# A filter's results through DRAM: loads of two units in 16 rows of 32 KB, stores in pieces of 512 bytes

## The chip, the core and the metric

The kernel runs on one core of one Trainium2 chip. The metric is the device time of one execution in microseconds. Three runs of the kernel before took 3746.42, 3749.2 and 3750.16 us; the median is 3749.2 us.

## The reference, cut to what matters

The input is one sequence of 2048 rows by 1024 columns. Two kinds of layer alternate, each behind a layer norm and added to its input:

```python
x = x + A(layernorm(x), wqkv, wo)      # attention, 32 heads
x = x + B(layernorm(x), w_r, w_i)      # spectral filter
x = x + A(layernorm(x), wqkv, wo)
x = x + B(layernorm(x), w_r, w_i)

def B(x, w_r, w_i):
    X = rfft2(x, axes=(-2, -1))
    y = irfft2(X * (w_r + 1j * w_i), s=(S, D), axes=(-2, -1))
    return y
```

The change lies in the filter B, which is executed twice.

## The kernel before, in words

Attention (lines 343 to 988) takes most of the time and is not touched. The filter is the function `spectral`, from line 1004. It does the two-dimensional transform by matrix products on TensorE (PE), in three stages.

The first stage (t1 and fa, lines 1034 to 1069) transposes 128-column blocks and multiplies by a matrix that does the small outer factors of the transform at once. Its result lies in SBUF in the buffer of 64 KB per partition that the attention calls big or R (the two change places between the layers).

The second stage is a software pipeline over 32 units, the list UNITS of line 23. A unit is a pair of a column parity g (0 or 1) and a row frequency class k1, with four or five column classes. Units 0 to 15 have g = 0, and units 16 to 31 have g = 1. Iteration i of the loop at line 1216 holds, in this order:

- `fb(i)`, line 1130: the products of the forward row transform (L1122), and the copies of the result from PSUM into a tile B on ScalarE (L1115)
- `halves(i - 2)`, line 1176: ScalarE and VectorE split the filtered unit into two float16 parts, H (L1179, L1180)
- `fc(i - 1)`, line 1144: the forward column transform (L1154), the multiplication with the filter weights on VectorE and GpSimd (L1161 to L1169), and at its end `loadw(i + 2)` (L1089), a load of weights w, 256 KB as a rule
- `binv(i - 3)`, line 1182: the inverse row transform (L1122 again, from H), copied into U by ScalarE (L1115)
- `turn(i - 6)`, line 1207: two loads of 128 KB from the DRAM tensor zt into the tile turned (L1210)
- `cinv(i - 4)`, line 1193: the inverse column transform (L1199, L1202), a copy from PSUM into a tile T on ScalarE (L1204), and the store of T to zt, 256 KB (L1205). There are three buffers of T
- in odd iterations, a load of 512 KB of the residual y (L1235)

Behind the loop stand `turn(30)` and `turn(31)`. In this loop the instructions of PE, ScalarE (ACT) and SyncE (SP) are issued in the order of the code. All loads and stores named here are issued by SyncE, which works through its queue in order: an instruction that has to wait for a semaphore holds up all behind it. VectorE (DVE) and GpSimd (POOL) get their order from the planner.

The way through DRAM is a transposition. In T, a partition stands for (r, q): r is one of two halves, q one of 64 column positions, and each partition holds four column classes j of 128 row positions n. In turned, a partition stands for a row of the third stage's matrix (`row`, line 32: unit, r and j), and holds 64 q of 128 n. The matrix `mi`, made by `spec_consts` at line 36, is laid out by the same function `row`.

The third stage (lines 1246 to 1296) multiplies turned by mi (`ai`, L1249). `even(a)` needs the half with g = 0, `odd(a)` the half with g = 1, so the first `odd` product needs the last loads of zt. VectorE (L1259, L1266, L1267) and GpSimd (L1268) add the results to the residual. In the second filter each of the eight steps stores 1 MB of the output, in pieces of 512 bytes (L1293, L1296). In the first filter the weights of the next attention are loaded and split in between (L312, L218, L219, L321 to L323).

Attention's partial sums go through GpSimd's DMA queue (L765 to L770): transfers of 32 neighbouring partitions, added up in DRAM.

Of the kernel before, what the change touches and what calls it, by code (L numbers as in the profile page):

```python
# [6 lines left out]
F32 = mybir.dt.float32  # L7
# [15 lines left out]
UNITS = [u for g in range(2) for u in  # L23
         [(g, k1, list(range(4 * h, 4 * h + 4))) for k1 in range(1, 8) for h in range(2)]
         + [(g, k1, [0, 1, 2, 3] if g else [1, 2, 3, 0, 4]) for k1 in (0, 8)]]
# [4 lines left out]


def row(i, r, j):
    return 32 * (i % 16 // 4) + 16 * r + 4 * j + i % 4


def spec_consts():
# [967 lines left out]
def spectral(nc, tc, ap, yd, xout, a, cst, zt, fast, flags=None, nxt=None, join=None):  # L1004
# [25 lines left out]
    turned = ap.r.rearrange("p (g q n) -> p g q n", g=2, q=64)  # L1030
# [99 lines left out]
    def fb(i):  # L1130
        g, k1, fs = UNITS[i]
        n = len(fs)
        pb = new_ps(n)
        for j, o, m in PAIRS[n]:
            src = [bh[:, g, i % 16, x] for x in range(2)] if fast else [bu[:, g, i % 16]]
            if j < 2:
                lr, li = ([v[:, r * n + o:r * n + o + m].rearrange("p a q -> p (a q)") for v in src] for r in range(2))
            else:
                lr, li = [v[:, 3:5].rearrange("p a q -> p (a q)") for v in src], None
            complex_mm(pb[j // 2][:64 * m, j % 2].rearrange("p r k -> p (r k)"), lr, li, const("cb", k1))  # L1140
        B = Bt[i] = p2.tile([128, 6, 128], F32, name="B")
        restack(n, pb, B)

    def fc(i):
        g, k1, fs = UNITS[i]
        n = len(fs)
        B, w = Bt.pop(i), W.pop(i)
        G = (p2 if fast else p3).tile([128, 2, 6, 64], F32, name="G")
        H = G if not fast else p3.tile([128, 2, 2, 6, 64], F16, name="H")
        Gt[i] = [H[:, x] for x in range(2)] if fast else [G]  # L1150
        for o, m in GRP[n]:
            pc = ps.tile([128, 4, 2, 64], F32, name="ps")
            for j in range(m):
                nc.tensor.matmul(pc[:, j].rearrange("p r f -> p (r f)"), B[:, POS[n][o + j]], C["cc"][:, 8 * g + fs[o + j]],  # L1154
                                 start=True, stop=True)
            xr, xi = pc[:, :m, 0], pc[:, :m, 1]
            wr, wi = w[:, 0, o:o + m], w[:, 1, o:o + m]
            p0 = POS[n][o]
            gr, gi = G[:, 0, p0:p0 + m], G[:, 1, p0:p0 + m]
            t_ = p1.tile([128, 2, 4, 64], F32, name="t_")  # L1160
            nc.vector.tensor_mul(gr, xr, wr)  # L1161
            nc.vector.tensor_mul(t_[:, 0, :m], xi, wi)
            nc.vector.tensor_mul(gi, xr, wi)
            last = nc.vector.tensor_mul(t_[:, 1, :m], xi, wr)
            if flags is not None and seen and o == 0:
                with tc.issue_after(last.ins):
                    largest(*seen.pop())
            nc.gpsimd.tensor_tensor(gr, gr, t_[:, 0, :m], op=ALU.subtract)
            nc.gpsimd.tensor_tensor(gi, gi, t_[:, 1, :m], op=ALU.add)  # L1169
            if fast:  # L1170
                todo.append([i] + [v[:, :, p0:p0 + m] for v in (G, H[:, 0], H[:, 1])])
        loadw(i + lead)
# [3 lines left out]
    def halves(i):  # L1176
        while todo and todo[0][0] == i:
            _, gs, hi, lo = todo.pop(0)
            nc.scalar.copy(hi, gs)  # L1179
            nc.vector.tensor_sub(lo, gs, hi)  # L1180
# [12 lines left out]
    def cinv(i):  # L1193
        g, k1, fs = UNITS[i]
        n = len(fs)
        U = Ut.pop(i)
        pt = ps.tile([128, 4, 128], F32, name="ps")
        for j in range(4 if n == 4 else 3):
            nc.tensor.matmul(pt[:, j], C["ci"][:, 8 * g + fs[j]], U[:, j], start=True, stop=True)  # L1199
        if n == 5:  # L1200
            for j in range(2):
                nc.tensor.matmul(pt[64 * j:64 * j + 64, 3], C["ci"][:, 8 * g + fs[3 + j], 0:64], U[:, 4 + j], start=True, stop=True)  # L1202
        t_ = p4.tile([128, 4, 128], F32, name="T")
        nc.scalar.copy(t_, pt)  # L1204
        nc.sync.dma_start(zt[i], t_)  # L1205

    def turn(i):
        for r in range(2):
            r0 = row(i, r, 0)
            nc.sync.dma_start(turned[r0:r0 + 13:4, UNITS[i][0]], zt[i][64 * r:64 * r + 64].rearrange("q j p -> j q p"))  # L1210

    for i in range(lead):
        loadw(i)
# [1 line left out]
    with tc.manual_schedule(engines=set(hold)) if fast else nullcontext():  # L1215
        for i in range(36):
            if i < 32:
                fb(i)
            if 0 <= i - 2 < 32 and fast:
                halves(i - 2)  # L1220
            if 0 <= i - 1 < 32:
                fc(i - 1)
            if 0 <= i - 3 < 32:
                binv(i - 3)
            if 0 <= i - 6 < 32:
                turn(i - 6)
            if 0 <= i - 4 < 32:
                cinv(i - 4)
            if i == 20 and join:
                joined = join(ps)  # L1230
            if 20 <= i < 23 and join:
                next(joined, None)
            if i % 2 and i < 32:
                t = i // 2
                nc.sync.dma_start(rest[:, t], yd[t * 128:(t + 1) * 128, :])  # L1235
        turn(30)
        turn(31)
    psum.close()
    work.close()
    mid.close()  # L1240
# [202 lines left out]
def build(nc, tc, a):  # L1443
    with ExitStack() as ctx:
        cp = ctx.enter_context(tc.tile_pool(name="consts", bufs=1))
        dr = ctx.enter_context(tc.tile_pool(name="layers", bufs=1, space=DRAM))
        cst = {n: cp.tile(s, d, name=n) for n, s, d in (
            ("ident", [128, 128], F32), ("ones", [128, 32], F32), ("bones", [128, 32], BF16),
            ("half", [128, 1], F32), ("sign", [128, 1], F32), ("mhalf", [128, 1], F32), ("mi", [128, 2, 128], F32))}
        nc.scalar.dma_start(cst["ident"], a["ident"])  # L1450
        nc.scalar.dma_start(cst["sign"], a["sign"])
        nc.vector.memset(cst["ones"], 1.0)
        nc.vector.memset(cst["bones"], 0.0)
        for h in range(4):
            nc.vector.memset(cst["bones"][32 * h:32 * h + 32, h:h + 1], 1.0)
        nc.vector.memset(cst["half"], 0.5)
        nc.vector.memset(cst["mhalf"], -0.5)
        flags = {
            "mv": cp.tile([128, 32, 2], F32, name="fmv"),
            "w": cp.tile([128, 32], F32, name="fw"),  # L1460
            "wb": cp.tile([128, len(UNITS)], F32, name="fwb"),
            "r": cp.tile([128, 16], F32, name="fr"),
            "st": cp.tile([128, NST, 2, 6], F32, name="fst"),
            "bad": cp.tile([1, 1], I32, name="fi"),
        }
        nc.vector.memset(flags["r"], 0.0)
        x1 = dr.tile([2048, 1024], F32, name="x1")
        zt = dr.tile([32, 128, 4, 128], F32, name="zt")
        ap = AttnPools(tc)
        ap.open_small()  # L1470
        x = a["x"]
        for o in (0, 512):
            nc.sync.dma_start(ap.x[:, 0, o:o + 512], x[0:128, o:o + 512])
        wts = [Weights(nc, ap, a["wp"], True, [flags["w"][:, i:i + 1] for i in range(32)], []),
               Weights(nc, ap, a["wp"], None, [], [])]
        for layer in range(2):
            y = dr.tile([2048, 1024], F32, name=f"y{layer}")
            attention(nc, tc, layer, ap, x, y, wts[layer], a["wo"], cst, dr, flags)
            x = a["out"] if layer else x1
            if layer:  # L1480
                spectral(nc, tc, ap, y, x, a, cst, zt, True, join=lambda ps: combine_flags(nc, ps, cp, flags, cst))
            else:
                spectral(nc, tc, ap, y, x, a, cst, zt, True, flags, (s for ph in PH0 for s in wts[1].prep(ph)))
        ap.close()
        bad = nc.values_load(flags["bad"][0:1, 0:1], min_val=0, max_val=1)
        with tc.If(bad > 0):
            x = a["x"]
            for layer in range(2):
                y = dr.tile([2048, 1024], F32, name=f"gy{layer}")
                general_attention(nc, tc, x, y, a["wp"], a["wo"], cst)  # L1490
                ap = AttnPools(tc)
                load_norm(nc, tc, cst, ap, y)
                x = a["out"] if layer else x1
                spectral(nc, tc, ap, y, x, a, cst, zt, False)
                ap.close()
# [28 lines left out]
```

## Time and profile before

| what | value |
|---|---|
| median of three runs | 3749.2 us |
| the profiled execution's own time | 3747.77 us |
| its span, first to last instruction | 3745.9 us |
| mean granted PE clock | 0.988 |
| PE busy in the span | 97% |
| loads of zt in the two filters, 128 KB each | 64 and 64 |
| stores of T, 256 KB each | 64 |
| second stage, first filter: first matmul to last T copy | 1645.13 to 1831.84 us |
| second stage, second filter: first matmul to last T copy | 3520.89 to 3686.63 us |

The profile is one execution. Its times count from the first instruction of the span. A row of a timeline has the start, the time taken, the engine, the line, the operation, the tiles (out<-in) and how many instructions are merged; in square brackets stands the idle time ahead of it and what ended it. A row of a wait reads: the engine and its line, what it waited for, microseconds in total, number of times, the longest. A DMA share is the mean busy share of the core's 16 DMA engines; it can exceed 1 because a DMA engine works on more than one packet at a time. An issue of a DMA (SPq) is the time for which the queue's engine was busy issuing, not the time of the transfer.

### The profile page before, as it was taken

How to read it: one execution, taken by the hardware profiler on the slowest of the kernel's cores; microseconds unless marked ns; L12 is line 12 of the kernel's file. 1: busy time of each engine (PE TensorE's matmuls, PEld its weight loads, DVE VectorE, ACT ScalarE, POOL GpSimd, SP SyncE). 2: the span in 40 equal slices, each digit the busy share in tenths (PEclk: the TensorE clock that was granted, in tenths of full speed). 3: DMA queues.
4: the chain of work that ended last, by engine and by line, in shares of the span. 5: the costliest groups of instructions: out<-in, count | busy, mean ns of one | idle time of the engine just before them, and what ended most of it. 6: DMA issues, size and time to landing. Idle time of an engine off the chain costs nothing. (4 is left out here: it accounts for less than half of the span.)

```text
span 3745.9 us, 80372 instructions
## 1 busy us (share of the span) xinstructions
PE 3619.1 (97%) x32663; PEld 1600.1 (43%) x32663; DVE 3129.2 (84%) x3754; ACT 2900.8 (77%) x3571; POOL 671.0 (18%) x802
## 2 busy tenths in 40 slices
PE   8999999999999999998689999999999999999995
PEld 5333433443343333487654334333433433333885
DVE  7799899989999979875467998999899889788744
ACT  5788888888888868577447888888888888676782
POOL 1012112211121100124220111111111111000243
PEclk9999999999999999999889999999999999999998
DMA  7122332222233432245451222323222334321465
GB/s 196 21 52 55 54 56 48 60 42 52 55 64 60 95 102 74 81 141 182 140 158 27 52 52 51 55 53 60 44 52 52 63 59 97 102 77 74 145 208 177
DMA packets 245965, 307.74 MB, mean 82 GB/s; under 512 B 77392, under 2 KB 156752, under 8 KB 244560
## 3 DMA queue, kind: packets, MB, share of 16 engines
q1 hardware_dynamic: 206624, 228.49, 19.4%
q0 software_dynamic: 37632, 73.43, 13.7%
q8 instruction: 258, 4.23, 0.5%
q14 instruction: 123, 1.01, 0.1%
q10 hardware_dynamic: 1328, 0.59, 0.1%
HBM read 165.65 MB, written 135.20 MB: 80 GB/s over the span
## 5 line engine op out<-in xcount | busy, mean ns | idle before, releaser
L740 ACT ACTIVATE p<-s,bias 128x1024 f32<-128x1024 f32 x2048 | 2170.9, 1112 | 457.7 <-PE s L736 439.6
L759 DVE TENSOR_TENSOR acc<-acc,p 128x1024 f32<-128x1024 f32 x896 | 1044.0, 1220 | 55.9 <-ACT p L740 54.8
L759 DVE TENSOR_TENSOR big<-big,p 128x1024 f32<-128x1024 f32 x448 | 522.5, 1221 | 38.4 <-ACT p L740 37.2
L759 DVE TENSOR_TENSOR R<-R,p 128x1024 f32<-128x1024 f32 x448 | 522.2, 1220 | 31.4 <-ACT p L740 29.8
L746 PE MATMUL o<-p,big 128*32 128x512 f32 x4096 | 492.5, 598 | 0.0
L746 PE MATMUL o<-p,R 128*32 128x512 f32 x4096 | 492.5, 598 | 0.0
L426 PEld LDWEIGHTS <-wqk 128*128 128x128 f16 x3072 | 275.7, 98 | 418.8 <-issue 127.3
L426 PE MATMUL x<-R,wqk 128*128 128x512 f16 x1440 | 338.1, 380 | 1.9 <-ACT big L488 1.2
L426 PE MATMUL x<-big,wqk 128*128 128x512 f16 x1440 | 338.2, 380 | 1.4 <-ACT R L488 0.7
L736 PEld LDWEIGHTS <-R 32*128 32x128 f16 x6144 | 114.8, 92 | 370.6 <-issue 312.8
L736 PEld LDWEIGHTS <-big 32*128 32x128 f16 x6144 | 114.2, 92 | 370.2 <-issue 312.0
L746 PEld LDWEIGHTS o<-p,R 128*32 128x32 f32 x4096 | 106.8, 109 | 261.7 <-issue 261.7
L746 PEld LDWEIGHTS o<-p,big 128*32 128x32 f32 x4096 | 106.8, 109 | 261.7 <-issue 261.7
L736 PE MATMUL s<-R 32*128 32x512 f16 x3072 | 213.8, 377 | 0.1
L736 PE MATMUL s<-Q,big 32*128 32x512 f16 x3072 | 212.7, 377 | 1.0 <-DVE mqk L460 1.0
L736 PE MATMUL s<-Q,R 32*128 32x512 f16 x3072 | 212.6, 378 | 1.0 <-DVE mqk L460 1.0
L736 PE MATMUL s<-big 32*128 32x512 f16 x3072 | 212.6, 377 | 0.1
L765 POOL DMA_DIRECT2D zd<-acc x112 | 92.4, 825 | 650.7 <-DVE z L775 304.2
L484 PE MATMUL x<-wv,big 128*128 128x256 f16 x1392 | 166.7, 276 | 3.0 <-DVE R L219 2.2
L484 PEld LDWEIGHTS <-big 128*128 128x128 f16 x1536 | 146.2, 99 | 49.7 <-issue 28.6
L484 PE MATMUL x<-wv,R 128*128 128x256 f16 x1392 | 165.7, 275 | 0.7 <-ACT R L392 0.7
L484 PEld LDWEIGHTS <-R 128*128 128x128 f16 x1536 | 145.7, 98 | 46.7 <-issue 26.1
(524 smaller groups left out, 4158.6 us busy)
## 6 DMA issues: line engine op xcount, KB each, us to landing
zd<-acc POOLq DMA_DIRECT2D x112, 256.0 KB, 4.1
wst<-in_wp SPq DMA_DIRECT2D x96, 256.0 KB
zt<-T SPq DMA_DIRECT2D x64, 256.0 KB
w<-in_w SPq DMA_DIRECT2D x60, 256.0 KB
zd<-R POOLq DMA_DIRECT2D x56, 256.0 KB, 4.1
zt<-zr SPq DMA_DIRECT2D x224, 64.0 KB
od<-ohl SPq DMA_DIRECT2D x56, 256.0 KB
zd<-big POOLq DMA_DIRECT2D x56, 256.0 KB, 4.1
```

Of the source, the lines that this page charges most:

```text
L426: nc.tensor.matmul(ps, a, b, start=i == 0, stop=i == 23)
L484: nc.tensor.matmul(ps[:, j], x[c][:, d, o:o + 128], w[:, n, d], start=i == 0, stop=i == 23)
L736: nc.tensor.matmul(s[h // 2][:, h % 2], K[g][r, a, kt * 128:kt * 128 + 128], Q[g][r, b, c * 512:c * 512 + 512], start=i == 0, stop=i == 2)
L740: nc.scalar.activation(p, s[hf], AF.Exp, bias=bias[g], scale=SCALE / (SQ * SQ))
L746: nc.tensor.matmul(O[g, c][32 * h:32 * h + 32], V[g][:, kt, 32 * h:32 * h + 32], P[g, c, kt, h // 2][:, h % 2], start=kt == 0, stop=kt == ...
L759: last_add = nc.vector.tensor_add(a, a, p)
L765: nc.gpsimd.dma_start(z, a[32 * j:32 * j + 32].rearrange("p a j n -> p (a j n)"), max_dma_last_dim=2048, **({"accum_op": ALU.add} if j els ...
```

## The change

In zt, the class j now stands ahead of the partition p. A store therefore writes four pieces of 512 bytes for each partition, where it wrote one of 2 KB. `row` is numbered anew, so that the rows of two neighbouring units are 16 neighbouring partitions, in the order in which zt holds them. A load then takes two units at once: 16 rows, each of 32 KB in one piece, on both sides. It is issued in odd iterations from 7 on, for units i - 7 and i - 6, and once behind the loop. Before, a load took four rows, each gathered from 64 pieces of 512 bytes, for one half r of one unit.

```diff
 def row(i, r, j):
-    return 32 * (i % 16 // 4) + 16 * r + 4 * j + i % 4
+    return 8 * (i % 16) + 2 * j + r
...
         nc.scalar.copy(t_, pt)
-        nc.sync.dma_start(zt[i], t_)
+        nc.sync.dma_start(zt[i].rearrange("j p n -> p j n"), t_)
 
     def turn(i):
-        for r in range(2):
-            r0 = row(i, r, 0)
-            nc.sync.dma_start(turned[r0:r0 + 13:4, UNITS[i][0]], zt[i][64 * r:64 * r + 64].rearrange("q j p -> j q p"))
+        r0 = row(i, 0, 0)
+        nc.sync.dma_start(turned[r0:r0 + 16, UNITS[i][0]],
+                          zt[i:i + 2].rearrange("i j (r q) n -> (i j r) q n", q=64))
...
-            if 0 <= i - 6 < 32:
-                turn(i - 6)
+            if 7 <= i and i % 2:
+                turn(i - 7)
...
         turn(30)
-        turn(31)
...
-        zt = dr.tile([32, 128, 4, 128], F32, name="zt")
+        zt = dr.tile([32, 4, 128, 128], F32, name="zt")
```

## The prediction

> **What bounds the kernel now.** I read the page first: its span, and the chain of waits summed by line.
>
> ```profile
> span 3745.9 us, 80372 instructions
> PE ps L1122 1%; DMA zt<-T 1%; PE ps L1053 1%; PE ps L1154 1%; PE ps L1038 1%; PE ai L1249 0%; PE ps L1199 0%; DMA w<-in_w 0%; POOL R L1268 0%; ACT B L1115 0%; DMA big<-zt 0%; ACT U L1115 0%; SPq L1210 0%; ACT H L1179 0%; DVE e L1266 0%
> ```
>
> Most of the kernel is attention, which the change does not touch. The chain's visible part is the second filter, and there the stores zt<-T rank next to TensorE's largest line: the round trip through zt is on the path. The waits say where it bites, for the second filter (3520 to 3703) and then the first (1640 to 1862).
>
> ```profile
> ACT T L1204 <- DMA zt<-T: 18.1, 11, 4.3
> ```
>
> ```profile
> ACT T L1204 <- DMA zt<-T: 41.9, 23, 4.8
> ```
>
> The copy of a unit's result into T cannot start until one of three T buffers has been stored. The wait occurs 11 times in one filter and 23 times in the other. The stretches (columns: busy of PE, PEld, DVE, ACT, POOL, the PE clock, DMA share, GB/s) tell whether the DMA engines as a whole are short.
>
> ```profile
> 3590.00:3610.00 20.00, 20.00 (x179) 17.57 (x177) 11.38 (x28) 18.51 (x51) 10.69 (x16) 1.00 0.65 206
> 3539.00:3540.00 1.00, 1.00 (x12) 0.98 (x11) 0.00 (x0) 0.96 (x3) 0.00 (x0) 1.00 1.05 393
> ...
> 3697.00:3701.20 4.20, 0.00 (x0) 0.00 (x0) 0.00 (x0) 0.00 (x0) 0.00 (x0) 0.50 0.28 85
> 3712.50:3715.50 3.00, 3.00 (x29) 3.00 (x29) 2.91 (x4) 1.01 (x1) 2.50 (x1) 1.00 1.05 291
> ```
>
> They are not: 0.65 busy in mid-stage. But from 3697.0 to 3701.2 only the last loads of zt run, at a share of 0.28 and 85 GB/s, while the output stores, also in pieces of 512 bytes, run at 1.05 and 291. So these loads keep about 0.28 / 1.05 x 16 = 4 of the 16 engines busy, which fits a load of four rows. The transfer rate in forty slices of 3590 to 3610 shows the same comb in mid-stage: bursts near 300, then plateaus near 87 where only those four work.
>
> ```profile
> GB/s 267 99 89 88 87 226 353 243 313 98 88 122 86 84 274 305 208 313 251 414 315 225 87 87 87 321 283 243 284 112 91 95 84 87 326 301 295 344 295 279
> ```
>
> SyncE's queue in that stretch, over two units:
>
> ```profile
> 3607.13 0.39 SPq L1089 DMA_DIRECT2D w<-in_w  x1
> 3607.62 1.28 SPq L1210 DMA_DIRECT2D big<-zt  x2
> 3608.99 3.21 SPq L1205 DMA_DIRECT2D zt<-T  x1
> 3612.31 0.37 SPq L1089 DMA_DIRECT2D w<-in_w  x1
> 3612.78 1.48 SPq L1210 DMA_DIRECT2D big<-zt  x2
> 3614.35 2.38 SPq L1205 DMA_DIRECT2D zt<-T  x1
> 3616.83 0.38 SPq L1235 DMA_DIRECT2D R<-y  x1
> 3617.32 0.39 SPq L1089 DMA_DIRECT2D w<-in_w  x1
> ```
>
> It issues without a gap, and a pair of units takes 3617.32 - 3607.13 = 10.19 us. The store, which needs little to issue by itself, sits there for 3.21 and 2.38 us right behind the loads: the four engines' queues are full. In the first filter a pair takes 1794.01 - 1782.21 = 11.80 us.
>
> ```profile
> 1782.21 0.38 SPq L1089 DMA_DIRECT2D w<-in_w  x1
> ...
> 1794.01 0.57 SPq L1089 DMA_DIRECT2D w<-in_w  x1
> ```
>
> TensorE would go faster. Its first matmuls of a unit (L1122 from cb) start, for the first, the 22nd and the last two of 32 units, at these times; the last row is the first product that needs the last loads.
>
> ```profile
> 3520.89 0.71 PE L1122 MATMUL ps<-cb,R 128*128 128x256 f16 x5
> ```
>
> ```profile
> 3609.78 1.47 PE L1122 MATMUL ps<-cb,R 128*128 128x256 f16 x12
> ...
> 3652.60 1.47 PE L1122 MATMUL ps<-cb,R 128*128 128x256 f16 x12
> ...
> 3657.01 1.47 PE L1122 MATMUL ps<-cb,R 128*128 128x256 f16 x12
> ...
> 3703.39 21.84 PE L1249 MATMUL ai<-mi,big 128*128 128x128 f32 x173 [11.25 <-issue]
> ```
>
> An undisturbed unit takes 4.41 us (3652.60 to 3657.01), 8.82 a pair, against the queue's 10.19. PE ran ahead for 21 units (88.9 us) on its buffers; then the T buffers ran out.
>
> **The change, part by part.** *The loads.* Four loads a pair, 256 pieces each, become one of 16 rows of 32 KB. What counts is how long it holds the engines. Bounds: at the 291 GB/s of the output stores 512 KB take 1.8 us. Its rows go to 16 neighbouring partitions, which no load here does; the nearest row is GpSimd's partial sums (L765), which read 32 neighbouring partitions.
>
> ```profile
> zd<-acc POOLq DMA_DIRECT2D x112, 256.0 KB, 4.1
> ...
> zd<-zd POOLq DMA_DIRECT2D x56, 64.0 KB, 2.6
> ```
>
> The 192 KB more cost 1.5 us: 131 GB/s. At that rate 512 KB take 4.0 us; if half the partitions mean half the rate, 8.0 us. I take 4.0, since that row is the only one for a compact block, and keep 1.8 and 8.0. [...]
>
> *The stores.* 128 pieces of 2 KB become 512 of 512 bytes: 256 KB at 291 instead of 393 GB/s (the stretch at 3539, a store alone) is 0.90 instead of 0.67 us of the engines. The issue need not grow: the output's store of 2048 pieces issues in 0.39 us where nothing blocks it.
>
> ```profile
> L1293 SPq DMA_DIRECT2D out<-R x7: 372/388/1991, 3711.4 to 3731.8; - x7
> ```
>
> *The queue.* A pair now issues two w (0.37 each), one load (0.64, half of 1.28), two stores (0.39 each), one y (0.38) and some 0.6 of semaphores: 3.1 us of PE's 8.82. A load now waits for two stores, and the next store, y and w are queued behind that wait, with ACT's T copies and the filter multiply waiting for them. It costs nothing in the loop: the younger store was issued two iterations (8.8 us) before and lands in about 2.6 - 0.2 + 0.9 = 3.3 us (the 64 KB row less its data, plus its own). Were a store to take over 8.8 us, SyncE would stall.
>
> *The engines.* A pair needs 1.8 us for the stores, 2.7 for w and y (1 MB at 393), 4.0 for the load: 8.5 us, just under 8.82. So PE sets the pace, and the T waits go.
>
> **The sum.** Second filter: the last unit's first matmul comes at 3609.78 + 10 x 4.41 = 3653.9, against 3657.01: 3.1 us. Then the drain. The first unit, with nothing blocked, needed 3537.47 - 3520.89 = 16.6 us from first matmul to T; the last one today 3686.04 - 3657.01 = 29.0.
>
> ```profile
> 3537.47 0.59 ACT L1204 COPY T<-ps 128x512 f32<-128x512 f32 x1
> ```
>
> ```profile
> 3686.04 0.59 ACT L1204 COPY T<-ps 128x512 f32<-128x512 f32 x1 [4.29 <-DMA zt<-T]
> ```
>
> I take 16, since PE has less beside it: 13.0 us. Last, from the T copy to the first product of the second half: 17.35 us today. New: copy 0.6; the load of units 28 and 29, started some 1 us later, holds the engines for 4.0; the last store behind it 0.9 and an estimated 1.4 to land; then the last load, 2.4 fixed (2.6 - 0.2), 4.0 of data, and 0.4 to PE: 14.7, so 2.7 us. Sum 18.8 us. The rest shifts unchanged: the output stores already fill the engines (1.05).
>
> First filter, with the same steps; it starts at 1645.13, so the last unit's first matmul moves from 1797.74 to 1645.13 + 88.9 + 44.1 = 1778.1: 19.6 us.
>
> ```profile
> 1645.13 0.71 PE L1122 MATMUL ps<-cb,big 128*128 128x256 f16 x5
> ...
> 1797.74 1.47 PE L1122 MATMUL ps<-cb,big 128*128 128x256 f16 x12
> ```
>
> ```profile
> 1831.25 0.59 ACT L1204 COPY T<-ps 128x512 f32<-128x512 f32 x1 [4.77 <-DMA zt<-T]
> ```
>
> ```profile
> 1851.73 21.32 PE L1249 MATMUL ai<-mi,R 128*128 128x128 f32 x176 [15.75 <-DMA R<-zt]
> ```
>
> Drain 33.5 to 16: 17.5. T to product 20.5 to 14.7: 5.8; less an estimated 1.5 because the next layer's weights, whose ACT work stands before the filter's there, now queue behind a load on all engines. Sum 41.4. Together 60 us. The profiled execution took 3747.77 us (span and 1.9 around it), so 3688; the median of the runs, 3749.2, is 1.4 higher: **3689 us**.
>
> **The rivals.** *The engines take PE's place.* If the load runs halfway between the pool's 131 and today's 85 GB/s, 108, it takes 4.9 us, a pair 9.4, 0.55 behind PE. Over 16 pairs that is 9 us a filter, and with two loads in the tail 2 more: 22 of the 60 go, 3711. For it: the sum of 8.5 has little room. Against: the three T buffers hide some of the lag. [...]
>
> *Slower.* With the 8.0 us load a pair takes 12.5 us, longer than today's 10.19 and 11.80; this decides from loads of 5.7 us on in the second filter, 7.3 in the first. Price: 16 x 2.3 + 16 x 0.7 = 48, and two longer loads in each tail, about 5 a filter: 3749 + 58 = 3807. For it: all 16 engines would be held where now twelve stay free. Against: GpSimd's row includes an accumulation that a load lacks.
>
> *No change.* ACT is 18.51 of 20 us busy; if it cannot hold 4.41 once SyncE stops pacing it, the stage stays: 3749. Against: 21 units ran at that pace.
>
> *A smaller gain elsewhere.* VectorE's and GpSimd's order is planned and may come out otherwise behind the first filter, losing its tail (23 us): 3712.
>
> **How the numbers follow.** Forecast 0.62, engines 0.22, planned order 0.06: faster 0.90. No change 0.04. Slower 0.06. Within 0.2% (7.5 us) is about what a measurement of this kernel cannot tell from nothing. Low end: with a load of 1.8 us two loads less in each tail, 9 us, a drain of 14.5 saves 3, and TensorE, idle for a shorter time before the products, may run them above the 0.50 clock shown, 4 or so more a filter: 3669. The high end reaches past the engines' case to a load of 5.1: 3718.
>
> **What would show it.** Right: the T waits gone from both filters; SyncE's stores at about 0.39 us with gaps between issues; units 4.41 us apart to the end; no plateaus at 87 GB/s; the product 18 to 20 us earlier in the second filter and about twice that in the first. Wrong: a share near 1.0 at low GB/s while a load runs (the engines' case), or a pair longer than 10 us.

## The result and the profile after

The kernel after takes 3709.1 us (median of four runs, 3707.49 to 3711.67), against 3747.8 for the kernel before beside it (four runs, 3744.8 to 3750.16): 0.9898 of the time, interval 0.9881 to 0.9915. That is 38.7 us less. The forecast was 60 less, and the time lies at the figure of the first rival, 3711. The profiled execution took 3711.67 us, and its span is 36.1 us below that of before.

The page of after, first its span and then its chain of waits summed by line:

```profile
span 3709.8 us, 80239 instructions
PE o L746 24%; PE s L736 20%; PE x L426 16%; PE x L484 7%; PE x L547 6%; PE s L547 3%; DMA zt<-T 2%; PE ps L1122 2%; PE ps L1053 1%; PE ps L1038 1%; DVE acc L759 1%; PE ai L1248 1%; PE o L426 1%; DMA w<-in_w 1%; PE ps L1154 1%
```

The stores zt<-T are still on the path, now with 2% where it was 1%. Yet ScalarE hardly waits for them any more. The waits of the second filter (3490 to 3668), and then SyncE's own waits there (3480 to 3700):

```profile
ACT T L1204 <- DMA zt<-T: 5.8, 5, 2.0
```

```profile
SPq L1209 <- DMA zt<-T: 49.9, 14, 7.4
```

The wait for the T buffers went from 18.1 us to 5.8 (in the first filter from 41.9 to a single 0.65), as forecast. In its place SyncE waits 49.9 us in front of 14 of its loads, for the stores that the loads read. The first filter has the same wait 9 times, 24.5 us.

The stretches, with the columns as before (five engines, PE clock, DMA share, GB/s): the middle of the second filter, and the time in which only the last load runs.

```profile
3568.00:3618.00 50.00, 49.16 (x444) 44.85 (x443) 24.88 (x56) 43.51 (x111) 22.16 (x31) 1.00 1.01 209
3661.00:3665.70 4.70, 0.00 (x0) 0.00 (x0) 0.00 (x0) 0.00 (x0) 0.00 (x0) 0.50 0.75 112
```

This answers to the 0.65 at 206 GB/s of before. The bytes are the same, but now the DMA engines have no free time. And the single load of 512 KB moves in those 4.7 us, at 112 GB/s and a share of 0.75: that is 0.75 x 4.7 = 3.5 us of all 16 engines. Before, a load moved 85 GB/s, but held only 0.28 of them.

SyncE's queue over one pair of units, and the DMA issues of 3560 to 3610 (the last column is the median from issue to landing):

```profile
3599.09 0.32 SPq L1209 DMA_DIRECT2D big<-zt  x1
3599.50 0.38 SPq L1205 DMA_DIRECT2D zt<-T  x1
3599.97 0.46 SPq L1235 DMA_DIRECT2D R<-y  x1
3600.54 0.37 SPq L1089 DMA_DIRECT2D w<-in_w  x1
3601.02 0.68 SPq L1205 DMA_DIRECT2D zt<-T  x1
3604.16 0.33 SPq L1089 DMA_DIRECT2D w<-in_w  x1
3609.22 0.32 SPq L1209 DMA_DIRECT2D big<-zt  x1
```

```profile
w<-in_w SPq DMA_DIRECT2D x10, 256.0 KB, 10.1
zt<-T SPq DMA_DIRECT2D x10, 256.0 KB, 9.8
big<-zt SPq DMA_DIRECT2D x5, 512.0 KB, 9.7
```

Issuing no longer paces anything: the stores issue in 0.38 us at the median where they sat for 2.38 and 3.21. But a pair takes 3609.22 - 3599.09 = 10.13 us, as long as before, since everything lands 10 us after its issue. The chain of waits shows the loop that this makes:

```profile
3599.50 9.66 DMA zt<-T
...
3609.64 9.38 DMA zt<-T
...
3619.49 9.35 DMA zt<-T
```

A load waits for the store that was issued right behind the load before it. That store moves behind a load that holds the engines, and lands 9.4 to 9.7 us later; only then does the next load go out. The period is that landing and the 0.4 us of the load's issue. (Between two stores the chain names a T copy, which waits for the same landing.)

### The profile page after: what moved, and what is told of

It reads as the page before. It is cut to its first block, busy times and chain, and to the rows that moved or that the text cites. A ratio compares the mean times of both kernels' runs of the same rounds, so it can differ in the third digit from the quotient of the medians.

```text
span 3709.8 us, 80239 instructions
## 1 busy us (share of the span) xinstructions
PE 3606.5 (97%) x32663; PEld 1595.9 (43%) x32663; DVE 3128.7 (84%) x3754; ACT 2899.0 (78%) x3571; POOL 664.0 (18%) x802
## 4 chain that ended last, share of the span: by engine, by line
PE 84%; DVE 4%; DMA 4%; issue 4%; ACT 3%; POOL 1%; SPq 0%; DVEq 0%; ACTq 0%; POOLq 0%
PE o L746 24%; PE s L736 20%; PE x L426 16%; PE x L484 7%; PE x L547 6%; PE s L547 3%; DMA zt<-T 2%; PE ps L1122 2%; PE ps L1053 1%; PE ps L1038 1%; DVE acc L759 1%; PE ai L1248 1%; PE o L426 1%; DMA w<-in_w 1%; PE ps L1154 1%
```

## The experiments

Two theories could explain a load of 112 GB/s. **P**: the rate comes from where the rows go, 16 neighbouring partitions. **L**: it comes from the rows' length, pieces of 32 KB of which each is one packet (after's trace has 16 of 32768 bytes for a load). The first of the nine kernels makes transfers alone; the others differ from the kernel after as shown. Times stand beside those of the kernel before on the same chip.

**Transfers by themselves.** Loads of 512 KB, four of each form, one after the other: 16 rows of 32 KB to neighbouring partitions (L30), to every 8th (L33) and to every 4th (L36); 16 rows of 8 KB, four times (L40); 128 rows of 4 KB (L43); and two forms with four rows a load (L49, L56).

> This kernel leaves the whole computation out: it copies the input to the output, and ahead of that it makes the disputed transfers one at a time, each waited for, four times each. Theory P (partitions): a load of 16 rows of 32 KB is slow because its rows go to 16 neighbouring partitions. Then 512 KB to partitions 0 to 15 (near) land some 6.5 us after the issue, as the last load of the changed kernel did, and 512 KB to every 8th (far) or every 4th partition (mid) land in 4 to 5 us; four loads of 16 rows of 8 KB to partitions 0 to 15 (four) take 6.5 to 7.5 us together. Rival L (length): it is slow because each engine has one piece of 32 KB with nothing to overlap it. Then near, far and mid all take about 6.5 us, and four is faster than near. Both: 512 KB over 128 partitions (every) 3.5 to 4 us, the loads of the kernel before (old4) 8 us for 512 KB. A store in pieces of 512 bytes (pieces) takes 0.2 to 0.4 us longer than one in pieces of 2 KB (whole), some 3.3 us.

SyncE's queue; each load waits for the one before it:

```profile
33.37 0.33 SPq L30 DMA_DIRECT2D big<-in_x  x1
...
40.06 0.33 SPq L30 DMA_DIRECT2D big<-in_x  x1
...
46.66 0.33 SPq L30 DMA_DIRECT2D big<-in_x  x1
53.55 0.55 SPq L33 DMA_DIRECT2D big<-in_x  x1
...
58.45 0.51 SPq L33 DMA_DIRECT2D big<-in_x  x1
...
63.43 0.50 SPq L33 DMA_DIRECT2D big<-in_x  x1
```

To neighbouring partitions a load takes 6.6 to 6.7 us from issue to issue, to every 8th 4.9 to 5.0, in the same pieces of 32 KB and with a store beside each (the costlier form, 512-byte pieces, beside the faster loads: 291 GB/s in before, where 2 KB pieces had 393). Every 4th gave 4.8, the same as every 8th; 128 partitions 3.4 to 3.5. So the place of the rows matters, and the length of the pieces cannot be the whole. The loads of four rows took 7.6 to 7.9 in pieces of 32 KB, and 8.3 to 8.8 in pieces of 512 bytes. The four quarters of 8 KB rows took 4.5 us together, because each step waited only for its first quarter and the steps overlap. Just that makes them a measurement of the rate (columns: DVE, POOL, PE clock, DMA share, GB/s):

```profile
93.00:107.00 14.00, 0.46 (x3) 0.00 (x0) 1.00 0.95 115
```

With pieces a quarter as long, and with something always waiting, the engines are 0.95 busy at 115 GB/s. That is hardly more than the 112 of the long pieces, so L is out. The stores' forms could not be compared, since they ran beside the loads.

**The rows spread over the partitions** (spread8). The same load, but its rows go to every 8th partition:

```diff
-    return 8 * (i % 16) + 2 * j + r
+    return i % 16 // 2 + 8 * (8 * (i % 2) + 2 * j + r)
-        nc.sync.dma_start(turned[r0:r0 + 16, UNITS[i][0]],
+        nc.sync.dma_start(turned[r0:r0 + 121:8, UNITS[i][0]],
```

> The changed kernel, but the 16 rows of a load go to every 8th partition. Theory P: the load holds the engines for about 2.4 us in place of 4.7, a pair of units needs 2.4 + 4.5 = 6.9 us of the engines, less than TensorE's 8.82, so TensorE paces both filters to the end and the last loads land earlier: 3685 to 3695 us, 15 to 25 below the changed kernel. Rival L: as the changed kernel, 3705 to 3713. Rival Q (it is SyncE's wait for the younger store ahead of each load, and what is queued behind it, not the engines): 3703 to 3711.

It took 3689.5 us (3689.31 to 3690.95; before 3749.6): 0.9844, interval 0.9827 to 0.9860. The middle of its second filter, its DMA issues there, and SyncE's wait:

```profile
3560.00:3610.00 50.00, 50.00 (x454) 45.90 (x453) 25.61 (x58) 46.19 (x116) 23.94 (x34) 1.00 0.78 229
```

```profile
w<-in_w SPq DMA_DIRECT2D x12, 256.0 KB, 3.9
big<-zt SPq DMA_DIRECT2D x6, 512.0 KB, 6.0
...
zt<-T SPq DMA_DIRECT2D x11, 256.0 KB, 5.7
```

```profile
SPq L1209 <- DMA zt<-T: 6.8, 2, 4.6
```

With more bytes a second than in after, the engines are free for a fifth of the time; loads land in 6.0 us, stores in 5.7, all below the 8.82 of a pair; and PE is never idle. This is P, and it gives back 20 us by the rows' place alone. Why the place counts, no run here shows: by themselves, loads to every 8th and to every 4th partition measured the same, 4.8 to 5.0 us.

**The load cut in four by columns** (cut4): 16 rows of 8 KB to the same neighbouring partitions, four issues.

```diff
+        src = zt[i:i + 2].rearrange("i j (r q) n -> (i j r) q n", q=64)
+        for q in range(0, 64, 16):
+            nc.sync.dma_start(turned[r0:r0 + 16, UNITS[i][0], q:q + 16], src[:, q:q + 16])
```

> The changed kernel, but each load is cut into four of 16 rows of 8 KB, to the same neighbouring partitions. Theory P: the engines are held as long as before, 3707 to 3718 us (three more issues a pair, about 1 us of SyncE's time, which it has). Rival L: shorter pieces overlap, the load gets faster, 3688 to 3700. Rival Q: 3707 to 3718.

It took 3698.7 us (3698.23 to 3704.62; 0.9871, interval 0.9855 to 0.9888). By time alone that is L's number, not P's. The trace agrees that it isn't L: the middle of the second filter, the last loads, and the first product that needs them.

```profile
3560.00:3610.00 50.00, 50.00 (x454) 45.90 (x453) 26.11 (x60) 45.97 (x119) 23.76 (x34) 1.00 0.99 217
```

```profile
3651.28 1.69 SPq L1211 DMA_DIRECT2D big<-zt  x4
```

```profile
3654.35 24.11 PE L1249 MATMUL ai<-mi,big 128*128 128x128 f32 x192 [9.23 <-DMA big<-zt]
```

The engines are as full as in after (0.99 at 217 GB/s), and the pairs still come about 10 us apart. What is new is the end: the product starts 3.1 us after the first issue of the last loads. In after it takes 3667.04 - 3660.18 = 6.9. The first products read only the first quarter of the columns, and need not wait for the rest.

**The quarters issued last to first** (cut4rev): `for q in (48, 32, 16, 0):` in place of the loop above. The first product's quarter now comes last.

> The load cut in four as in the run cut4, which took 3698.7 us, some 10 less than the changed kernel; but the four are issued from the last quarter to the first. The engines have the same work in the same pieces. If cut4 gained because the first product of the second half needs only the first quarter of the rows (it started 3.1 us after the first of the last four loads was issued, against 6.9 us after the single load), the gain goes again where the first quarter comes last: 3705 to 3712 us. If shorter pieces make the loads themselves cheaper, it stays at 3696 to 3702.

It took 3702.8 us (3701.29 to 3708.14; 0.9885, interval 0.9870 to 0.9900), between the two expectations. The product starts 6.7 us after the first issue again, so about 4 us of the 10 that cut4 gains over after are the first quarter. The other 6 stay open. What the trace adds is that in cut4's stretch stores landed in 7.0 us, where after has 9.8, and that SyncE's wait for them in the second filter was 22.5 us in place of 49.9; no run tests whether that is the gain.

**Before's row numbers and loads, with the new layout of zt** (rows4): four loads of four rows of 32 KB for a pair.

```diff
-    return 8 * (i % 16) + 2 * j + r
+    return 32 * (i % 16 // 4) + 16 * r + 4 * j + i % 4
...
+        for u in (i, i + 1):
+            for r in range(2):
+                r0 = row(u, r, 0)
+                nc.sync.dma_start(turned[r0:r0 + 13:4, UNITS[u][0]], zt[u][:, 64 * r:64 * r + 64])
```

> The zt of the changed kernel with the loads of the kernel before: four loads a pair, each of four rows to every 4th partition, but each row is now one piece of 32 KB in place of 64 of 512 bytes; one part of the change alone. If four engines are what held the kernel before, the loads hold those four for 4 x 32 KB = 128 KB each, at the 159 ns per 4 KB that a load of long pieces takes there 5.1 us a pair in place of 6.0: a pair falls from 10.2 to about 9.3 us, and the time is 3722 to 3742. If the short pieces were what cost, it comes near the changed kernel, 3705 to 3715.

It took 3727.7 us (0.9944, interval 0.9924 to 0.9964): about half of the change's gain. SyncE's queue, and the middle of the second filter:

```profile
3602.32 4.47 SPq L1211 DMA_DIRECT2D big<-zt  x4
```

```profile
3560.00:3610.00 50.00, 48.97 (x425) 42.49 (x424) 24.16 (x66) 41.45 (x110) 21.61 (x34) 1.00 0.68 199
```

Here the engines have room (0.68), and SyncE is again held while it issues: 4.47 us a pair. So this part of the forecast's picture stands: loads of four rows, which left the engines at a share of 0.28 in before, hold up the issuing queue, and a load of 16 rows ends that (it issues in 0.32 us in after). The time met its range, but not by the expected step: a pair takes 10.4 us here (five from 3581.11 to 3632.90), not 9.3, and the gain lies in the first filter, where the way from the first unit to the product takes 187.0 us in place of 206.6.

**The store ahead of the load** (late). In each iteration the block `cinv(i - 4)` stands ahead of `turn(i - 7)`, so that the store for which the next load waits isn't queued behind a load. This tells the wait in SyncE's queue from the full engines.

> The changed kernel, but in each iteration the store of a unit is issued ahead of the load of an older pair, so that SyncE's wait for the younger store of that pair no longer stands before it. If it is that wait (49.9 us in the second filter) that costs, rather than the engines: 3685 to 3697 us. If the engines are the bound (busy at a share of 1.01), they have the same work: a pair still takes about 9.9 us, and only the chain of store, load, store, load at the end gets shorter, by about the 7 us of one round in each filter at most: 3698 to 3706.

It took 3698.3 us (3697.43 to 3699.17; 0.9870, interval 0.9855 to 0.9885), at the edge of what the engines' account gave. SyncE's wait for zt in the second filter is nearly gone, and yet the engines stay full or nearly so (a stretch of the first filter, then one of the second):

```profile
SPq L1209 <- DMA zt<-T: 5.9, 1, 5.9
```

```profile
1700.00:1780.00 80.00, 78.87 (x697) 70.17 (x695) 47.01 (x113) 70.85 (x185) 39.09 (x56) 1.00 0.99 219
3560.00:3610.00 50.00, 47.51 (x413) 42.81 (x411) 21.99 (x53) 42.56 (x109) 23.23 (x30) 0.97 0.95 211
```

So the store's place is worth some 11 us, and the full engines are not the effect of the wait. In the second filter the gain lies behind the units: from the last unit to the last T copy 15.8 us (24.0 in after), from there to the product 15.2 (18.6). The units themselves take longer, 138.3 us (134.7).

**Both** (spread8late): the rows spread, and the store ahead of the load.

> Rows on every 8th partition and the store ahead of the load. With the engines no longer short (share 0.75) the order matters only at the end, where store, load, store, load follow one another: 1 to 5 us a filter below the 3689.5 of the run spread8 by that: 3680 to 3689. If the wait for the younger store was still in the way in mid-stage, more: below 3680.

It took 3686.3 us (3683.82 to 3688.99; 0.9838, interval 0.9823 to 0.9853), 3 less than the spread alone, which the two intervals don't tell apart. The traces show two effects that nearly cancel. In the first filter the way from the first unit to the product is 6 us shorter (165.1 and 171.4); in the second it is 3 us longer (164.1 and 160.7), because there the units take 137.7 us in place of 133.25.

**A better version** (best). In spread8, three loads of the next layer's weights stood ahead of the last load of zt in the first filter's queue, and held it up for 8.47 us:

```profile
1803.02 8.47 SPq L312 DMA_DIRECT2D wst<-in_wp  x3
1811.58 0.48 SPq L1209 DMA_DIRECT2D R<-zt  x1
```

This kernel adds to spread8late that those loads are held until the last load of zt has been issued, and that this one load is cut in four, as in cut4:

```diff
+        step = 16 if i == 30 else 64
+        for q in range(0, 64, step):
+            d = nc.sync.dma_start(turned[r0:r0 + 121:8, UNITS[i][0], q:q + step], src[:, q:q + step])
...
+                with ap.tc.issue_after(LAST[-1].ins) if LAST and self.flag is None else nullcontext():
+                    nc.sync.dma_start(s, sl[len(st)][2].rearrange("p (d c) -> p d c", c=128))
```

> Rows on every 8th partition, the store ahead of the load, the last load of each filter cut in four so that the first product needs only a quarter of it, and in the first filter the loads of the next weights held behind the last load (in the run spread8 three of them stood ahead of it on SyncE's queue and took 8.5 us). Theory: the path from the last T copy to the first product of the second half falls from 11.7 to about 8 us in the second filter and from 17.7 to about 9 in the first: 3672 to 3683. Rival: TensorE is not ready earlier, or the weights then come too late for the steps behind: 3684 to 3690.

It took 3680.3 us (3679.02 to 3680.84; 0.9822, interval 0.9808 to 0.9835).

**Its order mended** (best2). With the store ahead of the load throughout, the second filter of best ran some 138 us from the first to the last unit, as it did in late and spread8late. So here the store goes ahead only in the last iterations, where the drain begins:

```diff
-            if 7 <= i and i % 2:
+            if 7 <= i < 30 and i % 2:
                 turn(i - 7)
             if 0 <= i - 4 < 32:
                 cinv(i - 4)
+            if 30 <= i and i % 2:
+                turn(i - 7)
```

> As the run best, but the store goes ahead of the load only from iteration 30 on; before that the load comes first, as in the changed kernel. In best and late the second filter took about 138 us from its first unit to its last, against 133 in spread8, with TensorE waiting once where the flags of the kernel are joined. If the order in mid-stage brought that about, the second filter is some 4 us shorter: 3674 to 3679. If not: 3679 to 3682, as best.

It took 3674.5 us (3673.54 to 3675.08; before 3748.6): 0.9804, interval 0.9790 to 0.9817. That is 74 us less than before, 35 more than the change brought. The first and the last unit of its second filter:

```profile
3473.57 0.71 PE L1126 MATMUL ps<-cb,R 128*128 128x256 f16 x5
...
3607.10 1.47 PE L1126 MATMUL ps<-cb,R 128*128 128x256 f16 x12
```

The units take 133.5 us, the pace that they have in spread8 (133.25).

## Why the prediction was right in sign, and its gain half again too large

The rows of after that answer to those on which the sum was built. The second filter (first, 22nd and last unit; the last T copy; the product), then the first filter (first and last unit, the last T copy, the product):

```profile
3489.85 0.71 PE L1122 MATMUL ps<-cb,R 128*128 128x256 f16 x5
...
3578.69 1.47 PE L1122 MATMUL ps<-cb,R 128*128 128x256 f16 x12
...
3624.51 1.47 PE L1122 MATMUL ps<-cb,R 128*128 128x256 f16 x12
...
3667.04 23.98 PE L1248 MATMUL ai<-mi,big 128*128 128x128 f32 x192 [14.09 <-DMA big<-zt]
```

```profile
3648.47 0.59 ACT L1204 COPY T<-ps 128x512 f32<-128x512 f32 x1 [2.02 <-DMA zt<-T]
```

```profile
1644.03 0.71 PE L1122 MATMUL ps<-cb,big 128*128 128x256 f16 x5
...
1781.57 1.47 PE L1122 MATMUL ps<-cb,big 128*128 128x256 f16 x12
...
1821.90 21.50 PE L1248 MATMUL ai<-mi,R 128*128 128x128 f32 x176 [13.30 <-DMA R<-zt]
```

```profile
1801.72 0.58 ACT L1204 COPY T<-ps 128x512 f32<-128x512 f32 x1 [0.65 <-DMA zt<-T]
```

| gain, us | first filter: forecast | measured | second filter: forecast | measured |
|---|---|---|---|---|
| first to last unit | 19.6 | 15.1 | 3.1 | 1.5 |
| last unit to T copy | 17.5 | 13.4 | 13.0 | 5.1 |
| T copy to product | 4.3 | 0.3 | 2.7 | -1.2 |
| sum | 41.4 | 28.8 | 18.8 | 5.3 |

The measured values are differences of the rows of before and after: in the second filter 133.0 was forecast from first to last unit, and it is 3624.51 - 3489.85 = 134.7. Some 2 us more lie outside the two filters' stages; 28.8 + 5.3 + 2.0 = 36.1.

**The step that failed** is "The engines. A pair needs 1.8 us for the stores, 2.7 for w and y (1 MB at 393), 4.0 for the load: 8.5 us, just under 8.82. So PE sets the pace". With the engines full, a pair takes 9.9 us in both filters (ten from 1684.61 to 1783.43, ten from 3539.03 to 3638.21). The traces keep every packet with its length and its duration. Added up by length over ten pairs of the second filter (in spread8 from 3515.20 to 3606.32), a pair took, in us of all 16 engines:

| part of a pair | forecast | after | spread8 |
|---|---|---|---|
| the load, pieces of 32 KB | 4.0 | 3.8 | 2.1 |
| two stores, pieces of 512 bytes | 1.8 | 2.5 | 1.9 |
| w and y, pieces of 2 to 4 KB | 2.7 | 3.6 | 3.0 |

So the load's own term holds. What was mis-sized are the others: their prices came from stretches in which no load to 16 neighbouring partitions ran, and beside it the stores cost 0.7 us a pair more and w and y 0.9. Beside the spread load the excess is 0.1 and 0.3. Why packets take longer beside the compact load stays open. That 4.0 fits is in part luck, since it comes from GpSimd's transfers, which fill twice as many partitions and add up in DRAM. By the clock, and not by the engines' time, after's last load took the 4.7 us of the row at 3661.

The rest of the sum was sound, as the second filter of spread8 shows, where the engines have free time:

```profile
3484.44 0.71 PE L1122 MATMUL ps<-cb,R 128*128 128x256 f16 x5
...
3617.69 1.47 PE L1122 MATMUL ps<-cb,R 128*128 128x256 f16 x12
...
3645.11 23.72 PE L1248 MATMUL ai<-mi,big 128*128 128x128 f32 x192 [4.61 <-DMA big<-zt]
```

```profile
3633.43 0.59 ACT L1204 COPY T<-ps 128x512 f32<-128x512 f32 x1 [0.46 <-ACT T L1204]
```

From first to last unit it takes 133.25 us (133.0 forecast), to the T copy 15.7 (16), to the product 11.7 (14.7). And the kernel's 3689.5 us is the time that was forecast for after, 3689.

**The second step that failed** hangs on it: the load's new wait "costs nothing in the loop", because the younger store "lands in about 2.6 - 0.2 + 0.9 = 3.3 us". It lands in 9.8. The prediction named the point, "Were a store to take over 8.8 us, SyncE would stall", and priced the store without the load in front of it on the same engines. In late, where the store stands ahead of the load, that was worth 11 us.

**Where the loss lies** was not foreseen by the rival either, although its price was close (a load of 4.9, 22 us off the gain). It set the lag at 0.55 us a pair, from first to last unit. But PE, which runs ahead on its buffers, still reaches its 22nd unit 3578.69 - 3489.85 = 88.84 us after the first, with nothing lost, and its last one only 1.7 late; the delayed stores and loads come due behind it. So 6 us of the loss lie between first and last units, where the rival put 18, and the rest behind them: that its price was close is in part luck. The end of the second filter's chain:

```profile
3646.21 6.67 DMA zt<-T
...
3653.38 6.74 DMA zt<-T
...
3660.18 6.50 DMA big<-zt
...
3667.04 13.28 PE ai L1248 x96
```

Two stores and a load, one behind the other, 6.5 to 6.7 us each. The forecast had a load of 6.4 there too, but only 2.3 for the last store.

**What held:** four rows keep about four of 16 engines busy, worked out from the 0.28 of before, and such loads held up SyncE (rows4 brings it back with 4.47 us a pair, after has 0.32); the T waits all but go; stores of 512 pieces issue in 0.38 us at the median; and the sign and the range. The sign that the prediction gave for "wrong", a share near 1.0 at low GB/s while a load runs, is what the profile shows in mid-stage.

**Open:** why the packets of the stores, w and y take longer beside the compact load, the 6 us of cut4 that its first quarter doesn't explain, and why the first filter's pairs took 11.80 us before where the second's took 10.19.

## What to carry to other kernels

Ask of a load two things: how many engines its rows keep busy, and which partitions they go to. The load that went from four rows to 16 but filled 16 neighbouring partitions moved only a third faster here (112 GB/s where it was 85) and left the other transfers no free engines (a share of 1.01 in mid-stage); a step of 8 between its partitions gave 20 us more. Price the other transfers as they run beside it, too: here the load's own term was right, and theirs grew. When a load waits for a store, price that store's landing behind whatever the same queue put in front of it, and look for a lag at the stage's end, behind the buffers that hide it; there, a last load cut so that its first reader needs only a part is cheap (cut4's product started 3.1 us after the first issue where after's took 6.9).

## What the runs showed of the hardware

To 16 neighbouring partitions the DMA engines moved 112 GB/s in pieces of 32 KB and 115 in pieces of 8 KB; a packet of 32 KB took 3.5 us at the mean in after's last load, and 2.0 in that of spread8. Busy engines did not mean more data: in the middle of the second filter all 16 were busy at a share of 1.01 with 209 GB/s, where the same traffic with spread rows needed 0.78 for 229. And the cost spread to the other transfers. With the compact load in the stream, the weights w, which have nothing to do with it, landed 10.1 us after issue; with the spread load it was 3.9.
